# One fused attention and feed-forward kernel: where four pieces of side work stand in the order that is issued

## The chip, the cores and the metric

One core of one Trainium2 chip runs the whole program. The metric is device time in microseconds (us) of one execution, the median of several. Five engines work side by side, each through its own queue in order: TensorE (PE, whose weight loads are shown as PEld), VectorE (DVE), ScalarE (ACT), GpSimd (POOL) and SyncE (SP), which here issues all DMAs.

## The reference

`reference()` is causal attention followed by a gated feed-forward layer, all in float32:

```
scores = q @ k.T / sqrt(64); scores[future] = -1e9       # 4 batches, 12 heads, 448 tokens, 64 wide
x = (softmax(scores) @ v), heads side by side            # 1792 tokens x 768
xn = x / sqrt(mean(x*x) + 1e-6) * rms_g
g, val = xn @ w_gate, xn @ w_val                         # 768 -> 1536, twice
out = (g * sigmoid(g) * val) @ w_out                     # 1536 -> 768
```

The feed-forward weights come as 64-bit floats and are brought to float32 on the chip.

## The kernel before, in words

The tokens are worked on in three groups: 512 tokens (group 0), 512 (group 1) and 768 (group 2). Every product of the feed-forward part is made of three matmuls on split operands, high times high, high times low and low times high; a split is a copy that rounds (on ACT) and a subtraction (on DVE or POOL).

The program is issued by hand in small steps. `post(delay, fn)` puts a piece of work `delay` ticks later, `tick()` ends a tick, and what stands in an engine's queue is what these calls put there, in that order; nothing reorders it.

- Round 0 (`w_ = 0`): the feed-forward part of group 0, with the attention of group 1 strewn between.
- Round 1 (`w_ = 1`, us 258 to 532 of the profile): the feed-forward part of group 1, 36 units of 3 ticks each, so 108 ticks of six matmuls of 512 columns; the attention of group 2 is strewn between. That attention is 18 rounds of two attention units, each round 5 steps: a visit (scores of two later units, products with v of two earlier ones), then four steps `some(e)`, for two units and e = 0, 1: three or four transposes into the one PSUM bank `t` (L247) and the copy `pt` out of it (L251 on DVE, L253 on ACT). The 90 steps are spread evenly over the first `AT[1]` ticks, so where there are more steps than ticks, some ticks get two.
- Beside it in round 1, for each of 12 pairs of weight units, `quad_sums` (L405 to L408) makes four sums in place on DVE, in the tiles `w_r` that `split_w` (ACT `w_h`, then POOL `w_l`) reads first, and stores them to DRAM (L412). It is posted `T["ws"]` ticks after the split of the second unit.
- The chain of x (`x_steps`) starts on the tick after the attention's last: column sums, `rc`, diagonals `dg`, a matmul that spreads them, twelve scalings of the tiles `xq` (L514, DVE), sums `t` of them (L523, DVE), and the split of seven operands `ch`, `cl`. `todo` holds it, one entry per tick. The products for group 2 need all of it.
- The products with the gate and value weights for group 2 (`quad_product`, us 532 to 665), 7 instead of 8 products per weight, by sums of blocks.
- The last stage (us 665 to 746): 7 times 3 products with w_out (`out_product`), 18 matmuls of 384 columns each, results in a ring of two banks `s` or in held banks `m`, `x`. `out_result` reads a bank on DVE (L705) or ACT (L703); `h_operand` makes the next left operand `oh`, `ol`; `wo_load` brings w_out tiles in (L655, three DMAs each, four buffers) and `wo_split` splits them into `a_h` (ACT) and `a_l` (DVE).

Of the kernel before, what the change touches and what calls it, by code (L numbers as in the profile page):

```python
# [14 lines left out]
ALU = mybir.AluOpType  # L15
# [23 lines left out]
        for g in range(NG) for c in range(NP)}  # L39
# [1 line left out]
MASKED = -8.0e9  # L41


T = dict(c0=0, c1=1, c2=4, c20=9, c3=5, c30=10, c5=7, c50=14, exp=1, exp0=3, gt=1, hh=1, hl=4, ws=4,
         ld=4, ld1=11, lv=5, norm0=7, norm1=2, r1=5, so=3, wl=2, wl0=8, xl=2, xl0=9)
LOAD = (4, 12, 24, 36, 48, 60, 74)
CONVERT = (20, 32, 44, 62, 76)
# [3 lines left out]
WR = 4  # L51
WARM = [9, 0, 0, 2]
EXTRA = 4
AT = [108, 74]
XT = 768
HX = XT // 2
RING = 6
# [4 lines left out]
def attention_ffn(ctx: ExitStack, tc: tile.TileContext, qk0, qk1, qk2, v, v2, w, g, out, out2):  # L62
# [7 lines left out]
    nc = tc.nc  # L70
# [59 lines left out]
    def post(delay, fn):  # L130
        if delay <= 0:
            fn()
        else:
            later.setdefault(now[0] + delay, []).append(fn)
# [97 lines left out]
    def steps_t(p):  # L232

        if not 0 <= p < len(UNITS):
            return []
        _, kind, _, _, _, _ = UNITS[p]
        pr = hs[p]
        kb = KB[kind]

        def some(e):  # L240
            pt = pr["pt", e] = pt_p.tile([P, W], F32, tag=f"pt{e}", name="pt")
            ps = bank("x" if e and p < ENDS[1] + 1 else "t")
            at = 0
            for j in range(NKB[kind]):
                for o, wd in blocks(kind):
                    if kb * j < wd:
                        nc.tensor.transpose(ps[:kb, at: at + P],  # L247
                                            pr["sp"][e][:, o + kb * j: o + kb * (j + 1)], ident)
                        at += P
            if kind or (e and p < ENDS[0]):  # L250
                nc.vector.tensor_copy(pt[:kb, :at], ps[:kb, :at])  # L251
            else:
                nc.scalar.copy(pt[:kb, :at], ps[:kb, :at])  # L253

        return [lambda e=e: some(e) for e in (0, 1)]
# [146 lines left out]
    def quad_sums(v, t0, t1):  # L402

        a11, a12, a21, a22 = t0[:, : HX], t0[:, HX:], t1[:, : HX], t1[:, HX:]
        nc.vector.tensor_tensor(a22, a21, a22, op=ALU.add)  # L405
        nc.vector.tensor_tensor(a21, a11, a21, op=ALU.subtract)
        nc.vector.tensor_tensor(a11, a22, a11, op=ALU.subtract)
        nc.vector.tensor_tensor(a12, a12, a11, op=ALU.subtract)  # L408

        def store():  # L410
            for d, t in ((wy[v][:, : HX], a11), (wy[v][:, HX:], a22), (wz[v][:, : HX], a21), (wz[v][:, HX:], a12)):
                nc.sync.dma_start(out=d, in_=t)  # L412

        post(2, store)


    m_ps = {}
# [63 lines left out]
    xc = {}  # L481

    def x_steps():

        sm = side["sm"]
        rc = sm.tile([P, 6], F32, name="rc")
        dg = sm.tile([P, 2, HX], F32, tag="p2", name="dg").rearrange("p a (b c) -> p (a b) c", c=P)
        rb = {}

        def columns():  # L490
            ps = bank("t")[:, :6]
            for i in range(6):
                nc.tensor.matmul(ps[:, i: i + 1], acc[2, i // 3][:, P * (i % 3): P * (i % 3 + 1)],
                                 ones[:, :1], start=True, stop=True)
            nc.scalar.activation(rc, ps, AF.Sqrt, bias=eps, scale=1.0 / DM)
            post(1, lambda: nc.vector.reciprocal(rc, rc))

        def diagonal():
            for i in range(6):
                r = rc[:, i: i + 1]  # L500
                if i % 2:
                    nc.scalar.mul(dg[:, i], ident, r)
                else:
                    nc.gpsimd.tensor_scalar(dg[:, i], ident, r, 1.0, op0=ALU.mult, op1=ALU.mult)

        def spread():
            for j in (0, 1):
                rb[j] = bank("xy"[j])[:, :HX]
                nc.tensor.matmul(rb[j], ones, dg[:, 3 * j: 3 * j + 3].rearrange("p a b -> p (a b)"),
                                 start=True, stop=True)  # L510

        def scale(c, j):
            x = xr[2, c][:, HX * j: HX * (j + 1)]
            nc.vector.scalar_tensor_tensor(  # L514
                out=x, in0=x, scalar=g_sb[:, c: c + 1], in1=rb[j], op0=ALU.mult, op1=ALU.mult)

        tmp = {}

        def blk(k, j, c):
            return xq[c][:, k, HX * j: HX * (j + 1)]  # L520

        def sub(dst, a, b):
            nc.vector.tensor_tensor(dst, a, b, op=ALU.subtract)  # L523

        def sums(c):
            t12 = sm.tile([P, 2, HX], F32, tag=f"p{c}", name="t12")
            t1, t2 = t12[:, 0], t12[:, 1]
            t4 = sm.tile([P, HX], F32, tag=f"t4{c}", name="t4")
            sub(t1, blk(0, 1, c), blk(0, 0, c))
            sub(t2, blk(1, 1, c), t1)  # L530
            sub(blk(0, 1, c), blk(1, 1, c), blk(0, 1, c))
            sub(t4, blk(1, 0, c), t2)
            tmp[c] = t1, t2, t4

        def operand(i, c):
            if c == 0:
                xc[i] = tuple(side["xc"].tile([P, 3, HX], F32R, name=f"{n}{i}") for n in ("ch", "cl"))
            t1, t2, t4 = tmp.get(c, (None,) * 3)
            src = (blk(0, 0, c), t2, blk(1, 0, c), t1, blk(0, 1, c), blk(1, 1, c), t4)[i]
            split(xc[i][0][:, c], xc[i][1][:, c], src, i not in (0, 2, 5))  # L540

        todo = [[columns], [], [diagonal], [], [spread], []]
        for c in range(3):
            todo.append([lambda c=c, j=j, q=q: scale(q, j) for q in (c, c + 3) for j in (0, 1)])
            todo.append([lambda c=c, i=i: operand(i, c) for i in (0, 2, 5)])
        todo += [[lambda c=c: sums(c)] for c in range(3)]
        todo += [[lambda i=i, c=c: operand(i, c) for c in range(3)] for i in (1, 3, 4, 6)]
        return todo


# [98 lines left out]
    def wo_load(n):  # L649
        if n >= 21:  # L650
            return
        i, sl = divmod(n, 3)
        t = wr_p.tile([P, 2, 3, P], F32, tag="w", name="w_o")
        for m in range(3):
            nc.sync.dma_start(out=t[:, :, m], in_=WSRC[i](m).rearrange("p (k m) -> p k m", m=P)[  # L655
                :, 2 * sl: 2 * sl + 2])
        wt["o", n] = t

    def wo_split(n):
        if n >= 21:  # L660
            return
        f2["o", n] = ring(8 * NF // 2 + n)
        split(*f2["o", n], wt["o", n].rearrange("p a b c -> p (a b c)"), True)
# [99 lines left out]
    with tc.manual_schedule():  # L763
# [145 lines left out]
        for q in range(1, 4):  # L909
            h_operand(q)  # L910
        wo_split(5)
        for q in range(21):
            i, p = divmod(q, 3)
            ps_ = out_product(i, p)
            out_result(i, p, ps_)
            h_operand(q + 4)
            wo_load(3 * (i + 2) + p)
            if p == 2:
                for n in range(3):
                    wo_split(3 * (i + 2) + n)  # L920


# [46 lines left out]
```

## Time and profile before

| | |
|---|---|
| runs of before | 754.33, 757.47, 756.74 us; median 756.74 |
| profiled execution | 751.23 us, of which its span (first to last instruction) is 749.2 |
| mean granted TensorE clock in it | 0.974 of full speed |
| busy shares | PE 91%, weight loads 74%, DVE 71%, ACT 50%, POOL 49% |
| DMA | 138.80 MB, mean 185 GB/s |

Busy times of engines are counted in the span; a value in square brackets at the end of an instruction's row is the time its engine idled before it, and who released it. A granted clock of 1.00 is 2.4 GHz, 0.50 is 1.2 GHz.

### The profile page before, as it was taken

How to read it: one execution, taken by the hardware profiler on the slowest of the kernel's cores; microseconds unless marked ns; L12 is line 12 of the kernel's file. 1: busy time of each engine (PE TensorE's matmuls, PEld its weight loads, DVE VectorE, ACT ScalarE, POOL GpSimd, SP SyncE). 2: the span in 40 equal slices, each digit the busy share in tenths (PEclk: the TensorE clock that was granted, in tenths of full speed). 3: DMA queues.
4: the chain of work that ended last, by engine and by line, in shares of the span. 5: the costliest groups of instructions: out<-in, count | busy, mean ns of one | idle time of the engine just before them, and what ended most of it. 6: DMA issues, size and time to landing. Idle time of an engine off the chain costs nothing. (4 is left out here: it accounts for less than half of the span.)

```text
span 749.2 us, 11965 instructions
## 1 busy us (share of the span) xinstructions
PE 682.7 (91%) x4106; PEld 556.4 (74%) x4106; DVE 535.4 (71%) x1023; ACT 373.0 (50%) x832; POOL 369.1 (49%) x319
## 2 busy tenths in 40 slices
PE   8798899999999978879789889997999999998877
PEld 5465677777778655656566667875999999998877
DVE  5976899999987657566667656275386767698662
ACT  6868777778745443434235343334333343354340
POOL 4987345556666336263546455686254534411010
PEclk9999899999999999999899999998999999999898
DMA  8645677877785565555465645314557576443431
GB/s 276 230 154 171 203 257 248 282 255 267 253 309 177 159 219 151 179 164 185 153 190 180 199 160 151 121 57 133 176 190 256 177 251 232 138 127 104 118 95 63
DMA packets 71355, 138.80 MB, mean 185 GB/s; under 512 B 7744, under 2 KB 39232, under 8 KB 71296
## 3 DMA queue, kind: packets, MB, share of 16 engines
q1 hardware_dynamic: 71296, 138.05, 56.4%
q8 instruction: 32, 0.52, 0.3%
q14 instruction: 27, 0.22, 0.1%
HBM read 104.21 MB, written 33.82 MB: 184 GB/s over the span
## 5 line engine op out<-in xcount | busy, mean ns | idle before, releaser
L207 POOL TENSOR_SCALAR sp<-sp,rs 128x384 f32<-128x384 f32 (+3 forms) x132 | 82.9, 646 | 127.9 <-DVE rs L211 123.1
L433 PE MATMUL m_ps<-xh,w_h 128*128 128x512 f32 x282 | 122.5, 434 | 3.0 <-DVE t_sb L457 3.0
L202 ACT ACTIVATE sp<-sp,nm 128x384 f32<-128x384 f32 (+3 forms) x168 | 87.5, 524 | 52.7 <-DVE nm L199 51.2
L435 PE MATMUL m_ps<-xh,w_l 128*128 128x512 f32 x282 | 113.3, 402 | 0.0
L434 PE MATMUL m_ps<-xl,w_h 128*128 128x512 f32 x282 | 112.9, 400 | 0.0
L102 POOL TENSOR_TENSOR a_l<-w_q,a_h 128x768 fp32r<-128x768 f32 x24 | 47.2, 1965 | 66.9 <-ACT a_h L473 66.8
L247 PE MATMUL t_ps<-ident,sp 128*128 128x128 f32 (+1 forms) x309 | 52.6, 283 | 27.6 <-DVE pt L251 14.4
L102 POOL TENSOR_TENSOR w_l<-w_r,w_h 128x768 fp32r<-128x768 f32 x36 | 71.5, 1994 | 12.1 <-ACT w_h L387 10.5
L247 PEld LDWEIGHTS t_ps<-ident,sp 128*128 128x128 f32 (+1 forms) x309 | 36.9, 140 | 47.2 <-POOL sp L207 18.9
L251 DVE COPY pt<-t_ps 128x384 f32<-128x384 f32 (+1 forms) x71 | 42.5, 599 | 37.8 <-PE t_ps L247 37.6
L273 PEld LDWEIGHTS a_ps<-pt,v_r 128*64 128x64 f32 (+1 forms) x864 | 40.9, 138 | 37.9 <-issue 13.4
L273 PE MATMUL a_ps<-pt,v_r 128*64 128x128 f32 (+2 forms) x864 | 56.4, 269 | 12.6 <-DVE pt L251 8.4
L433 PEld LDWEIGHTS m_ps<-xh,w_h 128*128 128x128 f32 x282 | 54.6, 194 | 14.5 <-DVE t_sb L457 3.0
L373 POOL TENSOR_SCALAR w<-w 128x768 f32<-128x768 f32 x36 | 43.9, 1219 | 40.9 <-ACT w_c L372 35.0
L435 PEld LDWEIGHTS m_ps<-xh,w_l 128*128 128x128 f32 x282 | 54.4, 193 | 12.6
L199 DVE CUSTOM_DVE_ANT_0 sp<-s_ps,mask 128x128 f32<-128x128 f32 (+3 forms) x136 | 49.9, 416 | 18.4 <-PE s_ps L190 17.5
L435 PE MATMUL m_ps<-hh,w_l 128*128 128x512 f32 x144 | 57.8, 401 | 4.8 <-POOL w_l L102 4.8
L434 PEld LDWEIGHTS m_ps<-xl,w_h 128*128 128x128 f32 x282 | 54.9, 195 | 8.1
L433 PE MATMUL m_ps<-hh,w_h 128*128 128x512 f32 x144 | 59.2, 411 | 0.0
L434 PE MATMUL m_ps<-hl,w_h 128*128 128x512 f32 x144 | 57.2, 397 | 0.0
L377 DVE SCALAR_TENSOR_TENSOR w_c<-w_c,w 128x768 int32<-128x768 int32 x36 | 51.2, 1422 | 0.5
L102 POOL TENSOR_TENSOR w_l<-w_c,w_h 128x768 fp32r<-128x768 f32 x18 | 40.0, 2222 | 22.5 <-ACT w_h L387 22.5
(178 smaller groups left out, 1698.4 us busy)
## 6 DMA issues: line engine op xcount, KB each, us to landing
w<-in_w SPq DMA_DIRECT2D x36, 768.0 KB, 5.2
w<-w_c SPq DMA_DIRECT2D x36, 384.0 KB, 2.6
w_r<-w SPq DMA_DIRECT2D x36, 384.0 KB, 4.7
qk_r<-in_qk SPq DMA_DIRECT2D x48, 256.0 KB, 4.4
qk_r<-in_qk SPq DMA_DIRECT2D x12, 512.0 KB, 5.9
v_r<-in_v SPq DMA_DIRECT2D x12, 448.0 KB, 4.5
v_r<-in_v SPq DMA_DIRECT2D x24, 192.0 KB, 3.1
wy<-w_r SPq DMA_DIRECT2D x24, 192.0 KB, 2.9
```

Of the source, the lines that this page charges most:

```text
L102: nc.gpsimd.tensor_tensor(out_, a, b, op=op)
L199: nc.vector.tensor_tensor_reduce(out=sp, in0=ps, in1=mk, scale=nsc, scalar=3.0e38, op0=ALU.add, op1=ALU.min, accum_out=nm)
L202: post(T["exp" if p >= ENDS[0] else "exp0"], lambda: nc.scalar.activation(sp, sp, AF.Exp, bias=nm, scale=-1.0, accum_out=sm))
L207: pr["norms"].append(lambda: nc.gpsimd.tensor_scalar(sp, sp, rs, 1.0, op0=ALU.mult, op1=ALU.mult))
L247: nc.tensor.transpose(ps[:kb, at: at + P], pr["sp"][e][:, o + kb * j: o + kb * (j + 1)], ident)
L251: nc.vector.tensor_copy(pt[:kb, :at], ps[:kb, :at])
L273: nc.tensor.matmul(av_ps[e * D: (e + 1) * D, p % 2, q0: q0 + n], raw_v[p][:kb, h, j, e, :], pr["pt", e][:kb, a0: a0 + n], start=(j == 0), ...
L373: (T["c1"], lambda: nc.gpsimd.tensor_scalar(hf_, hf_, 0.0, 1.0, op0=ALU.mult, op1=ALU.mult)),
L377: (T["c3" if s >= 5 else "c30"], lambda: nc.vector.scalar_tensor_tensor(out=ti, in0=ti, scalar=3, in1=lo, op0=ALU.logical_shift_left, op1= ...
L433: nc.tensor.matmul(ps, wh[:, k, :], mh, start=(first and k == ks[0]), stop=False)
L434: nc.tensor.matmul(ps, wh[:, k, :], ml, start=False, stop=False)
L435: nc.tensor.matmul(ps, wl[:, k, :], mh, start=False, stop=(last and k == 5))
```

## The change

Four edits, none of which adds or removes arithmetic.

1. `quad_sums` posts its four sums one a tick instead of issuing them together; `ws` goes from 4 to 3, so the first comes a tick sooner and the last two ticks later; the stores are posted after the last.
2. In group 2 the copies `pt` with e = 0 go to ACT (36 of 72); e = 1 stay on DVE.
3. `AT[1]` goes from 74 to 82, so group 2's attention takes 82 of the 108 ticks, and the chain of x starts 8 ticks later. Its entries are cut anew: operands are split one a tick beside the scalings and sums, not three in a tick.
4. In the last stage the w_out tiles of round i + 3 are loaded at the end of round i, after its splits; before, those of round i + 2 were loaded one at a time through round i.

```diff
-T = dict(... hl=4, ws=4,
+T = dict(... hl=4, ws=3,
-AT = [108, 74]
+AT = [108, 82]
...
-            if kind or (e and p < ENDS[0]):
+            if (kind and e) or (e and p < ENDS[0]):
                 nc.vector.tensor_copy(pt[:kb, :at], ps[:kb, :at])
             else:
                 nc.scalar.copy(pt[:kb, :at], ps[:kb, :at])
...
-        nc.vector.tensor_tensor(a22, a21, a22, op=ALU.add)
-        nc.vector.tensor_tensor(a21, a11, a21, op=ALU.subtract)
-        nc.vector.tensor_tensor(a11, a22, a11, op=ALU.subtract)
-        nc.vector.tensor_tensor(a12, a12, a11, op=ALU.subtract)
+        todo = [(a22, a21, a22, ALU.add), (a21, a11, a21, ALU.subtract),
+                (a11, a22, a11, ALU.subtract), (a12, a12, a11, ALU.subtract)]
+        for d, (o, x, y, op) in enumerate(todo):
+            post(d, lambda o=o, x=x, y=y, op=op: nc.vector.tensor_tensor(o, x, y, op=op))
...
-        post(2, store)
+        post(4, store)
...
-        for c in range(3):
-            todo.append([lambda c=c, j=j, q=q: scale(q, j) for q in (c, c + 3) for j in (0, 1)])
-            todo.append([lambda c=c, i=i: operand(i, c) for i in (0, 2, 5)])
-        todo += [[lambda c=c: sums(c)] for c in range(3)]
-        todo += [[lambda i=i, c=c: operand(i, c) for c in range(3)] for i in (1, 3, 4, 6)]
+        todo = [[columns], [], [diagonal], [], [spread], [], scales(0), scales(3),
+                scales(1) + op(0, 0), scales(4) + op(2, 0), scales(2) + op(5, 0), scales(5) + op(0, 1)]
+        for c, i, k in ((0, 2, 1), (1, 5, 1), (2, 0, 2)):
+            todo.append([lambda c=c: sums(c)] + op(i, k))
+        for i, x in ((1, op(2, 2)), (3, op(5, 2)), (4, []), (6, [])):
+            todo.append(op(i, 0) + op(i, 1) + op(i, 2) + x)
...
+        for n in (6, 7, 8):
+            wo_load(n)
         for q in range(21):
...
-            wo_load(3 * (i + 2) + p)
             if p == 2:
                 for n in range(3):
                     wo_split(3 * (i + 2) + n)
+                for n in range(3):
+                    wo_load(3 * (i + 3) + n)
```

On PE, in round 1, in the fourth of the 18 attention rounds, the six transposes of one unit (its halves e = 0 and e = 1) stood together; this is one piece of the difference.

```order
 L434 MATMUL m_ps<-xl,w_h 128x512
 L435 MATMUL m_ps<-xh,w_l 128x512
-L247 MATMUL t_ps<-ident,sp 128x128 x6
+L247 MATMUL t_ps<-ident,sp 128x128 x3
+L433 MATMUL m_ps<-xh,w_h 128x512
+L434 MATMUL m_ps<-xl,w_h 128x512
+L435 MATMUL m_ps<-xh,w_l 128x512
+L433 MATMUL m_ps<-xh,w_h 128x512
+L434 MATMUL m_ps<-xl,w_h 128x512
+L435 MATMUL m_ps<-xh,w_l 128x512
+L247 MATMUL t_ps<-ident,sp 128x128 x3
```

A tick's six matmuls now stand between the halves. Of the 18 rounds, four (the 4th, 6th, 13th and 15th) are parted so, and three more get a tick of matmuls at a place where the transposes had followed the visit, or the next visit them, at once; six rounds keep a pair of halves side by side.

On DVE, in the same stage, first before (the sums of the pair v = 3, in the fifth attention round), then of the change (the last sum of pair 2 and the first two of pair 3; all sums are line 408 there).

```order
L447 TENSOR_TENSOR gr<-m_ps,rms 128x512
L251 COPY pt<-t_ps 112x512
L405 TENSOR_TENSOR w_r<-w_r 128x384
L406 TENSOR_TENSOR w_r<-w_r 128x384
L407 TENSOR_TENSOR w_r<-w_r 128x384
L408 TENSOR_TENSOR w_r<-w_r 128x384
L211 RECIPROCAL rs<-sm 128x2 x2
L449 SCALAR_TENSOR_TENSOR t_sb<-t_sb,gr 128x512
L251 COPY pt<-t_ps 112x512 x3
```

```order
L408 TENSOR_TENSOR w_r<-w_r 128x384
L447 TENSOR_TENSOR gr<-m_ps,rms 128x512
L211 RECIPROCAL rs<-sm 128x2 x2
L449 SCALAR_TENSOR_TENSOR t_sb<-t_sb,gr 128x512
L251 COPY pt<-t_ps 128x384
L408 TENSOR_TENSOR w_r<-w_r 128x384
L447 TENSOR_TENSOR gr<-m_ps,rms 128x512
L251 COPY pt<-t_ps 128x384
L408 TENSOR_TENSOR w_r<-w_r 128x384
```

Four sums in a row ahead of the reciprocals and a copy have become single sums between them, and two of a round's four copies are gone from this queue.

On ACT, near the end of round 1, first before, then of the change: `w_h` is the split of a weight unit of round 1, `ch<-xq` and `ch<-t` are splits of the chain's operands (made of the scaled x and of its sums).

```order
L387 CAST w_h<-w_r 128x768
L473 CAST ch_5437<-xq 128x384 x3
L473 CAST ch_5451<-t_5358 128x384
L473 CAST ch_5451<-t_5371 128x384
L473 CAST ch_5451<-t_5390 128x384
L387 CAST w_h<-w_r 128x768 x2
```

```order
L473 CAST ch_5361<-xq 128x384
L387 CAST w_h<-w_r 128x768
L473 CAST ch_5471<-t_5419 128x384
L473 CAST ch_5471<-t_5434 128x384
L473 CAST ch_5471<-t_5449 128x384
L473 CAST ch_5379<-xq 128x384
```

Before, the last three `w_h` of the round stood behind splits that wait for the sums `t`; now the last `w_h` stands ahead of all of these.

## Rows read from the trace of the kernel before

**Rows 1.** Windows by stage: us; PE, PEld, DVE, ACT, POOL busy; clock; DMA share; GB/s.

```profile
258.00:476.90 218.90, 188.28 (x1458) 136.75 (x1458) 136.74 (x331) 87.75 (x215) 111.00 (x109) 0.98 0.53 171
476.90:531.80 54.90, 50.05 (x211) 40.28 (x210) 29.57 (x43) 19.34 (x37) 34.21 (x23) 0.94 0.34 108
531.80:665.40 133.60, 132.11 (x758) 130.81 (x757) 95.10 (x140) 54.57 (x90) 56.45 (x28) 1.00 0.61 201
665.40:745.60 80.20, 70.27 (x379) 69.05 (x377) 54.56 (x61) 29.73 (x42) 11.72 (x6) 0.94 0.33 97
```

**Rows 2.** Waits of PE, us 258 to 476.9: total, times, longest.

```profile
PE t_ps L247 <- DVE pt L251: 14.4, 10, 2.9
PE t_ps L247 <- POOL sp L207: 7.5, 6, 3.0
PE a_ps L273 <- DVE pt L251: 4.6, 1, 4.6
PE t_ps L247 <- DVE rs L211: 4.0, 3, 2.6
```

**Rows 3.** Timeline of PE, stalls of that stage: start, duration.

```profile
268.22 0.65 PE L247 MATMUL t_ps<-ident,sp 128*112 128x128 f32 x4 [3.03 <-POOL sp L207]
...
291.66 0.52 PE L247 MATMUL t_ps<-ident,sp 128*128 128x128 f32 x3 [2.63 <-DVE pt L251]
...
307.10 0.62 PE L247 MATMUL t_ps<-ident,sp 128*112 128x128 f32 x4 [2.77 <-DVE pt L251]
...
370.62 1.12 PE L273 MATMUL a_ps<-pt,v_r 128*64 128x128 f32 x8 [4.56 <-DVE pt L251]
```

**Rows 4.** Timeline of DVE ahead of the stall at 307.10.

```profile
303.30 0.55 DVE L405 TENSOR_TENSOR w_r<-w_r 128x384 f32<-128x384 f32 x1
...
305.06 0.56 DVE L408 TENSOR_TENSOR w_r<-w_r 128x384 f32<-128x384 f32 x1
...
306.27 0.68 DVE L251 COPY pt<-t_ps 112x512 f32<-112x512 f32 x1
```

**Rows 5.** Groups by line and shape: busy us, mean ns, idle before.

```profile
L251 DVE COPY pt<-t_ps 128x384 f32<-128x384 f32 x47 | 26.1, 554 | 26.5 <-PE t_ps L247 26.5
...
L406 DVE TENSOR_TENSOR w_r<-w_r 128x384 f32<-128x384 f32 x12 | 12.1, 1006 | 0.4
L253 ACT COPY pt<-t_ps 128x384 f32<-128x384 f32 x24 | 11.3, 469 | 7.8 <-PE t_ps L247 7.7
```

**Rows 6.** Waits of ACT, us 258 to 476.9.

```profile
ACT w_h L387 <- DMA w_r<-w: 21.2, 5, 6.0
ACT sq L304 <- POOL acc L102: 19.9, 4, 5.9
```

**Rows 7.** Timeline of POOL and PE, end of round 1.

```profile
511.30 9.18 POOL L102 TENSOR_TENSOR w_l<-w_r,w_h 128x768 fp32r<-128x768 f32 x3 [5.16 <-ACT w_h L387]
...
516.97 0.80 PE L435 MATMUL m_ps<-hh,w_l 128*128 128x512 f32 x1 [4.40 <-POOL w_l L102]
```

**Rows 8.** Timelines of DVE, PE and ACT, last stage.

```profile
694.10 0.96 DVE L475 TENSOR_TENSOR a_l<-w_o,a_h 128x768 fp32r<-128x768 f32 x1 [0.99 <-ACT a_h L473]
694.98 0.55 DVE L705 SCALAR_TENSOR_TENSOR u<-s_ps,m 128x384 f32<-128x384 f32 x1
...
729.71 0.96 DVE L475 TENSOR_TENSOR a_l<-w_o,a_h 128x768 fp32r<-128x768 f32 x1 [2.15 <-ACT a_h L473]
...
695.68 0.66 PE L572 MATMUL s_ps<-a_h,oh 128*128 128x384 f32 x1 [4.65 <-ACT oh L473]
...
731.29 0.66 PE L572 MATMUL s_ps<-a_h,oh 128*128 128x384 f32 x1 [5.03 <-ACT oh L473]
...
728.85 0.83 ACT L473 CAST a_h<-w_o 128x768 fp32r<-128x768 f32 x1 [2.37 <-DMA w_o<-wsum]
```

**Rows 9.** Windows behind two stalls: us, PE busy, granted clock, DMA share, GB/s.

```profile
371.00:374.00 3.00, 3.00 (x16) 0.50 1.00 309
517.00:520.60 3.60, 3.60 (x9) 0.50 0.70 207
```

More of the change, by code (lines that the diff above doesn't have):

```diff
@@ L41 @@
 MASKED = -8.0e9
-T = dict(c0=0, c1=1, c2=4, c20=9, c3=5, c30=10, c5=7, c50=14, exp=1, exp0=3, gt=1, hh=1, hl=4, ws=4,
+T = dict(c0=0, c1=1, c2=4, c20=9, c3=5, c30=10, c5=7, c50=14, exp=1, exp0=3, gt=1, hh=1, hl=4, ws=3,
          ld=4, ld1=11, lv=5, norm0=7, norm1=2, r1=5, so=3, wl=2, wl0=8, xl=2, xl0=9)
@@ L535, in operand @@
         def operand(i, c):
-            if c == 0:
+            if i not in xc:
                 xc[i] = tuple(side["xc"].tile([P, 3, HX], F32R, name=f"{n}{i}") for n in ("ch", "cl"))
@@ L540, in operand, with scales, op @@
             split(xc[i][0][:, c], xc[i][1][:, c], src, i not in (0, 2, 5))
-        todo = [[columns], [], [diagonal], [], [spread], []]
-        for c in range(3):
-            todo.append([lambda c=c, j=j, q=q: scale(q, j) for q in (c, c + 3) for j in (0, 1)])
-            todo.append([lambda c=c, i=i: operand(i, c) for i in (0, 2, 5)])
-        todo += [[lambda c=c: sums(c)] for c in range(3)]
-        todo += [[lambda i=i, c=c: operand(i, c) for c in range(3)] for i in (1, 3, 4, 6)]
+        def scales(q):
+            return [lambda j=j: scale(q, j) for j in (0, 1)]
+        def op(i, c):
+            return [lambda: operand(i, c)]
+        todo = [[columns], [], [diagonal], [], [spread], [], scales(0), scales(3),
[4 more added lines that the diff above has]
+            todo.append(op(i, 0) + op(i, 1) + op(i, 2) + x)
         return todo
```

## The prediction

> **What bounds the kernel now.** I read the busy shares by stage first. TensorE is busy 188.3 of 218.9 us in round 1, 50.1 of 54.9 at its end, 132.1 of 133.6 in the products for group 2 and 70.3 of 80.2 in the last stage [rows 1]. No other engine is near full in any of them, so the time is TensorE's own work and the places where TensorE stands still, and a change that adds no arithmetic can only work on the second. The waits of TensorE and its timeline give those places.
>
> In round 1 they come to 14.4 + 7.5 + 4.6 + 4.0 = 30.5 us [rows 2]. In most of them a set of transposes waits for the copy that empties the one bank `t`, or the products with v wait for such a copy. The stall of 2.77 us that ends at 307.10 shows the cause [rows 3]: the first of two adjoining sets was done, and DVE came to its copy only at 306.27, after four weight sums that ran from 303.30 to 305.62 [rows 4]. The 4.56 us that end at 370.62 have the same burst in front, lengthened: the second sum of a burst takes 1.006 us in the mean [rows 5], though one by itself takes 0.56 [rows 4].
>
> At the end of round 1 TensorE waits 4.40 us for POOL's low part of a weight, on which POOL had started after 5.16 us of waiting for ACT's high part [rows 7]. ACT had it behind splits of the chain of x, which waited for DVE's sums.
>
> In the last stage there are two stalls, 4.65 and 5.03 us [rows 8]. The rows name ACT's `oh`, but that operand had been ready; what ended last is DVE's reading of the ring bank (`u` at 694.98), and this stood behind the split of a w_out tile that waited 0.99 us for ACT, the second time 2.15 us; there ACT waited 2.37 us for the tile's DMA [rows 8].
>
> Behind a long stall the granted clock is 0.50 for some us [rows 9], so a stall can cost more than its own length: at half speed half of each busy us is lost.
>
> **The change part by part.** *Copies, sums and spacing in round 1 (edits 1, 2 and the 82 ticks).* These three meet the same 30.5 us, so they are costed together. A copy of 128x384 out of the bank takes 469 ns on ACT and 554 on DVE [rows 5], so 36 moved copies give DVE some 36 x 0.55 = 20 us of time back in a stage where it is busy 136.7 us, and cost ACT 17 where it is busy 87.8 [rows 1]. This is worth nothing by itself; what counts is when the copy comes. By kind:
>
> - Waits for DVE's copies, 14.4 + 4.6 = 19.0 us in 11 places [rows 2]. In four rounds the halves now have a tick of matmuls between them, which covers a copy; I take these as gone. At about seven places I leave the turn of one copy with its semaphores, about 0.7 us: an estimate from the copy's 0.554 [rows 5]. That leaves 4.9; recovered 14.
> - Waits for POOL's normalized scores and for DVE's reciprocals, 7.5 + 4.0 = 11.5 us in 9 places [rows 2]. This is a latency, scores to minimum to exponential to reciprocal to POOL. Three rounds get a tick more before the transposes that need it, the one with 3.03 us [rows 3] among them, and the reciprocals no longer stand behind bursts. I take 4.5 as recovered; the bounds are 0 and 8.
> - New waits. On ACT the copies stand behind what holds that queue: in this stage 5 waits of 21.2 us in all for a weight's DMA, and 4 of 19.9 us for POOL's accumulation [rows 6]. Going through the order of ACT, the copy of a round's second unit stands behind the second square in six of 18 rounds, and in two of them its transposes are a tick early; the waits for a DMA mostly end after a round's copies. The stores, and so the weights that reuse their buffers, come a tick later, but in the SP queue more weight loads now stand ahead of the loads of v that block it. With sums one tick sooner, DVE can also wait longer for POOL to have read the tile. I charge 3 us; the bounds are 0 and 12, the second being half the time that ACT is held, at the most part of one copy each.
>
> Sum 14 + 4.5 - 3 = 15.5. TensorE ran about 3 us at half clock behind the 4.56 us stall [rows 9], and somewhat behind another: 1.5 more if these stalls go.
>
> *Weight against the sums.* Bursts of 0.55 us instructions were stretched only while POOL ran: the mean of the second sum is 1.006 us [rows 5]. Spread out, each of the four meets POOL by itself, and POOL is busy 111.0 of 218.9 us [rows 1], so one or two of four will meet it, as now; I charge nothing beyond the 3 us. The Trainium skill, "SBUF — State Buffer", section "SBUF: two separate sides", says the ports that DVE and POOL share are an exclusive lock, held for a whole instruction. By that a spread burst can lose the lock up to four times where a burst mostly loses it twice: 11 bursts x 2 x 0.45 = 10 us more of DVE's time, an estimate, and if all of it reached TensorE, a gain of 16 in place of the sum's. The rows agree with it in kind.
>
> *The chain of x (edit 3).* It starts 8 ticks later and must be ready at the end of tick 108. A tick takes (54.9 - 4.4 - 1.8) / 33 = 1.5 us there [rows 1, 7, 9], so from its first entry at tick 84 there are 25 ticks, some 37 us; before, there were 33. DVE's part does not get shorter: twelve scalings and twelve sums, and its order is the same. What is gained is the order on ACT: the last `w_h` stands ahead of the splits that wait for the sums. POOL's last `w_l` still follows the last split of its operands, for which ACT waits for the sums of c = 2. I put that end at tick 106 or so, just when TensorE wants it, and leave 0.8 of 4.8 us: 4.0 recovered, bounds -3 and 4.8. Behind the 4.40 us stall 3.6 us were run at half clock [rows 9]: of the 1.8 lost, 1.5 back.
>
> *The w_out loads (edit 4).* The waits for DMA leave both chains: DVE's `u` or `c` comes 0.99 us sooner in the first stall and 2.15 in the second [rows 8], so 3.1 of 9.7. The rest stays: DVE has three `a_l` and ACT three `a_h` in front of the reading of the bank, and their order is unchanged. I add 0.3 for the clock. A load issued a round sooner needs a buffer whose split is a round old, so it doesn't block SP for long; the results' stores behind it are waited for by nobody until the end.
>
> Sum: 15.5 + 1.5 + 4.0 + 1.5 + 3.1 + 0.3 = 25.9 us. Against the profiled execution, 751.23, that is 725.3. That execution was 5.5 us faster than the median of the runs, 756.74, from which the forecast is taken: 756.74 - 25.9 = 730.8, so **731**.
>
> **The rivals.** *The copies on ACT come late.* Where ACT is held for a DMA or for POOL [rows 6], a copy behind it holds bank `t`, and TensorE. For it: 41 us of such holds. Against: most fall after a round's copies. At the upper bound 12 in place of 3, and with nothing recovered from the latency waits, 13.5 less: a gain of 12, **744**.
>
> *The stage is bound by its latency.* Each round goes scores, exponential, normalization, transposes, copy, products, and TensorE's wait moves to the next link when one is shortened. For it: waits for POOL and reciprocals are already 11.5 us, and two of the four in rows 2 are not for a copy. Against: the largest have a burst right in front. Then round 1 gives 3, the rest half of 9: a gain of 7, **750**. The change would then have done little of what it says.
>
> *The other side: sums that meet POOL one by one.* 44 sums stand in this stretch; if each waits for a POOL instruction as the second does now (1.006 against 0.56), DVE gets 44 x 0.45 = 20 us of waits, now in front of minima, reciprocals and the e = 1 copies in every tick instead of every third round, and a first sum that comes a tick sooner waits for `w_l`. It decides if more than some 60% of these 20 us reach TensorE on top of the old 30.5 with nothing recovered there; with the later chain of x costing 3: +12 + 3 - 3 = 12 slower, **769**. Short of that it only eats the gain.
>
> The lock of the Trainium skill's page named above is this rival's mechanism; the stretched rows bear it out for a burst, and none shows it for single sums.
>
> **How the numbers follow.** Forecast (722 to 740) 0.60, late copies (740 to 748) 0.20, latency (748 to 756) 0.13, the other side (over 757) 0.07. 8 in 10 lie between 721 and 750: the low end is the sum with the bounds of 8 for the latency waits and no new waits, 756.74 - 32.4 = 724, and a few us for the spread of the runs; the high end takes in the first two rivals. About 0.5% (3.8 us) is what a measurement can tell from no change; faster than 753: 0.60 + 0.20 + half of the third, 0.86; within: 0.08; slower: 0.06.
>
> **What would show it right or wrong.** Right: in the stage of round 1 TensorE's waits for L251 fall from 19 us to about 5, with a few small ones for ACT's L253; the 4.40 us wait for `w_l` falls under 1; the two stalls of the last stage are still there, of about 3.6 and 2.9 us, with no wait for a w_out DMA in front. Wrong: waits for L253 of 2 us and more behind a `w_h` or a square; sums of over 1 us in every place; a start of the group 2 products that waits for `cl`; stalls of the last stage that vanish or stay whole.

## The result, and the profile after

The changed kernel takes 729.25 us (median of 4 runs, 726.92 to 730.18), the kernel before in the same job 756.1 (4 runs, 754.33 to 757.47): a ratio of 0.9642, 95% interval 0.961 to 0.9673. The forecast was 731. The profiled execution took 730.18 us (span 728.1, clock 0.984) against 751.23, so the traces have 21.05 of the 26.9 us to show; the execution of before that was profiled was 5 us faster than its median.

Windows of the kernel after, by stage: us; PE, PEld, DVE, ACT, POOL busy; clock; DMA share; GB/s.

```profile
258.00:466.40 208.40, 196.56 (x1520) 144.08 (x1519) 116.18 (x303) 106.55 (x253) 119.37 (x114) 1.00 0.58 189
466.40:507.10 40.70, 35.89 (x161) 28.88 (x160) 29.07 (x39) 16.64 (x33) 24.80 (x19) 1.00 0.27 88
507.10:645.90 138.80, 134.22 (x757) 132.38 (x758) 98.42 (x144) 54.37 (x90) 57.46 (x28) 0.99 0.61 203
645.90:724.60 78.70, 72.06 (x379) 70.85 (x378) 54.45 (x62) 29.31 (x42) 11.73 (x6) 0.91 0.34 98
```

Against [rows 1], round 1 with its end is 24.7 us shorter (it ends at 507.1, not 531.8), the products for group 2 are 5.2 longer, the last stage 1.5 shorter. The first two windows can only be added: the attention now takes 8 more of the 108 ticks, so the border lies elsewhere in the work. The clock of 0.98 in round 1 is 1.00 now; that of the last stage fell from 0.94 to 0.91.

Waits of TensorE after, us 256 to 458.2, the attention's stretch of round 1: total, times, longest.

```profile
PE t_ps L247 <- ACT pt L253: 8.5, 11, 1.7
PE t_ps L247 <- POOL sp L207: 2.6, 3, 1.3
PE t_ps L247 <- DVE pt L251: 1.9, 2, 1.0
```

They answer to [rows 2]: 13.0 us in place of 30.5. None is longer than 1.7 us, and the waits of 2.6 to 4.6 us [rows 3] are gone. Of what is left, 8.5 us are for the copies that now run on ACT.

Groups of the weight sums, of before and then of after: busy us, mean ns, idle before.

```profile
L405 DVE TENSOR_TENSOR w_r<-w_r 128x384 f32<-128x384 f32 x12 | 10.2, 848 | 5.6 <-POOL w_l L102 5.6
L407 DVE TENSOR_TENSOR w_r<-w_r 128x384 f32<-128x384 f32 x12 | 8.3, 692 | 0.4
L408 DVE TENSOR_TENSOR w_r<-w_r 128x384 f32<-128x384 f32 x12 | 7.4, 615 | 0.4
```

```profile
L408 DVE TENSOR_TENSOR w_r<-w_r 128x384 f32<-128x384 f32 x48 | 32.9, 686 | 13.6 <-POOL w_l L102 9.0 <-DMA qk_r<-in_qk 2.6 <-DMA v_r<-in_v 1.7
```

With L406 of [rows 5] the 48 sums took 38.0 us in bursts. One at a time they take 32.9, a mean of 0.686 us: spread out they lost less to POOL, not more. (In either trace 12 of the 48 are stretched beyond 0.65 us, all of them beside a POOL instruction; in the bursts they were stretched further.)

Waits of ACT after, the same stretch, as in [rows 6].

```profile
ACT sq L304 <- POOL acc L102: 11.2, 4, 4.3
ACT w_h L387 <- DMA w_r<-w: 6.9, 4, 3.9
```

ACT is held for 18.1 us there, not 41.1.

Timeline of TensorE after: the stalls of over 2 us behind the attention (start, duration, in brackets the idle time before and its releaser).

```profile
500.88 0.50 PE L435 MATMUL m_ps<-hh,w_l 128*128 128x512 f32 x1 [2.50 <-POOL w_l L102]
...
507.16 0.66 PE L578 MATMUL m_ps<-ch,a_h 128*128 128x384 f32 x1 [2.37 <-DVE ob L441]
...
514.60 0.44 PE L578 MATMUL m_ps<-ch,a_h 128*128 128x384 f32 x1 [2.60 <-ACT m L601]
...
675.12 0.66 PE L578 MATMUL s_ps<-a_h,oh 128*128 128x384 f32 x1 [3.56 <-DVE u L711]
...
708.95 0.66 PE L578 MATMUL s_ps<-a_h,oh 128*128 128x384 f32 x1 [2.78 <-DVE c L711]
```

The first three stand where before there were 4.40 [rows 7] and 0.45 us: 7.47 in all, more than before. The third is already inside the products for group 2, and a stretch at half clock (below) lies there too: with 1.6 us for that, they are 4.2 of the 5.2 us by which the stage grew. The last two answer to [rows 8], 4.65 and 5.03 us.

Timeline of DVE after, chain of x.

```profile
477.63 0.69 DVE L441 SCALAR_TENSOR_TENSOR ob<-m_ps,rms 128x512 f32<-128x512 f32 x1 [9.25 <-PE m_ps L435]
...
495.56 7.81 DVE L475 TENSOR_TENSOR cl<-t,ch 128x384 fp32r<-128x384 f32 x6
503.29 3.12 DVE L475 TENSOR_TENSOR cl<-xq,ch 128x384 fp32r<-128x384 f32 x3
506.33 0.68 DVE L441 SCALAR_TENSOR_TENSOR ob<-m_ps,rms 128x512 f32<-128x512 f32 x1
506.94 1.48 DVE L475 TENSOR_TENSOR cl<-t,ch 128x384 fp32r<-128x384 f32 x3
508.34 0.95 DVE L475 TENSOR_TENSOR a_l<-w_q,a_h 128x768 fp32r<-128x768 f32 x1
```

Timeline of POOL after, the same place.

```profile
495.74 1.25 POOL L102 TENSOR_TENSOR cl<-xq,ch 128x384 fp32r<-128x384 f32 x1 [4.98 <-ACT ch L473]
497.40 1.34 POOL L102 TENSOR_TENSOR cl<-xq,ch 128x384 fp32r<-128x384 f32 x1 [0.41 <-ACT ch L473]
498.70 2.12 POOL L102 TENSOR_TENSOR w_l<-w_r,w_h 128x768 fp32r<-128x768 f32 x1
500.79 4.27 POOL L102 TENSOR_TENSOR a_l<-w_q,a_h 128x768 fp32r<-128x768 f32 x2
...
515.35 1.85 POOL L102 TENSOR_TENSOR a_l<-w_q,a_h 128x768 fp32r<-128x768 f32 x1 [10.29 <-ACT a_h L473]
```

What matters here is the overlap. From 495.74 to 505 POOL splits with one pause of 0.41 us, and DVE's six splits of sums, which take 0.49 us each in the three at 506.94, take 1.30 each, 7.81 in all. The result of the last tick, `ob` at 506.33, stands behind nine of them, and TensorE's first product for group 2 waits for it. The copy into `m`, the third wait, stands on ACT behind a split that waited for its tile's DMA:

```profile
513.65 0.51 ACT L473 CAST a_h<-w_q 128x384 fp32r<-128x384 f32 x1 [11.64 <-DMA w_q<-w]
```

Timeline of DVE after, last stage.

```profile
670.79 3.71 DVE L475 TENSOR_TENSOR a_l<-w_o,a_h 128x768 fp32r<-128x768 f32 x3 [0.88 <-ACT a_h L473]
674.43 0.54 DVE L711 SCALAR_TENSOR_TENSOR u<-s_ps,m 128x384 f32<-128x384 f32 x1
...
704.57 3.77 DVE L475 TENSOR_TENSOR a_l<-w_o,a_h 128x768 fp32r<-128x768 f32 x3
708.26 0.55 DVE L711 SCALAR_TENSOR_TENSOR c<-s_ps,u 128x384 f32<-128x384 f32 x1
```

No DMA stands in front of either stall any more. The bank's reading (`u`, `c`) stands behind three splits of w_out, and the rows of TensorE now name it.

The whole stretches at half clock, of after and then of the last stage of before: us; PE, PEld, DVE, ACT, POOL busy; clock; DMA share; GB/s.

```profile
506.94:510.35 3.41, 3.19 (x10) 3.22 (x11) 2.95 (x6) 0.00 (x0) 0.00 (x0) 0.50 0.64 193
674.19:681.01 6.82, 5.89 (x18) 5.92 (x19) 2.98 (x5) 0.08 (x1) 0.00 (x0) 0.50 0.62 163
708.32:715.15 6.83, 6.20 (x19) 6.23 (x20) 2.75 (x6) 0.00 (x0) 0.00 (x0) 0.50 0.16 58
```

```profile
693.70:700.52 6.82, 4.84 (x15) 4.88 (x16) 3.63 (x5) 1.84 (x3) 0.00 (x0) 0.50 0.64 179
731.24:734.66 3.42, 3.37 (x11) 3.40 (x12) 2.10 (x3) 0.00 (x0) 0.00 (x0) 0.50 0.32 115
```

Each begins inside a stall and outlasts it; TensorE then runs at 1.2 GHz. If half of its busy time there counts as lost (an estimate), that is 1.6, 2.9 and 3.1 us after, and 2.4 and 1.7 us in the last stage before.

### The profile page after: what moved, and what is told of

The parts are those of the page before. It is cut to its first block, busy times and chain, and to the rows that moved or that the text cites. A ratio compares the mean times of both kernels' runs of the same rounds, so it can differ in the third digit from the quotient of the medians.

```text
span 728.1 us, 11977 instructions
## 1 busy us (share of the span) xinstructions
PE 678.3 (93%) x4106; PEld 553.2 (76%) x4106; DVE 512.6 (70%) x987; ACT 387.6 (53%) x868; POOL 366.6 (50%) x319
## 5 line engine op out<-in xcount | busy, mean ns | idle before, releaser
L435 PE MATMUL m_ps<-xh,w_l 128*128 128x512 f32 x282 | 111.6, 396 | 0.0
L102 POOL TENSOR_TENSOR a_l<-w_q,a_h 128x768 fp32r<-128x768 f32 x24 | 48.8, 2034 | 65.8 <-ACT a_h L473 65.6
L102 POOL TENSOR_TENSOR w_l<-w_r,w_h 128x768 fp32r<-128x768 f32 x36 | 68.0, 1895 | 23.0 <-ACT w_h L387 22.3
L253 ACT COPY pt<-t_ps 128x384 f32<-128x384 f32 (+1 forms) x60 | 29.6, 494 | 44.0 <-PE t_ps L247 44.0
L102 POOL TENSOR_TENSOR w_l<-w_c,w_h 128x768 fp32r<-128x768 f32 x18 | 39.3, 2183 | 24.1 <-ACT w_h L387 21.3
L375 DVE SCALAR_TENSOR_TENSOR w<-w 128x768 int32<-128x768 int32 x36 | 46.3, 1287 | 6.8 <-POOL w L373 6.7
```

Of the source, the lines that this page charges most:

```text
L102: nc.gpsimd.tensor_tensor(out_, a, b, op=op)
L375: (T["c2" if s >= 5 else "c20"], lambda: nc.vector.scalar_tensor_tensor(out=lo, in0=lo, scalar=29, in1=hi, op0=ALU.logical_shift_right, op ...
L435: nc.tensor.matmul(ps, wl[:, k, :], mh, start=False, stop=(last and k == 5))
```

## The experiments

The theory: in round 1 the waits were copies behind bursts and tight spacing, and the three edits share the gain; at its end DVE's splits, slowed by POOL, took the place of the late weight; in the last stage the reading behind three splits remains. The rivals: one edit does it all; the entries of the chain do help and something else was lost; w_out loads do nothing. "Waits" below are TensorE's, from the profile of each run, in the attention's stretch and in the stretch of the chain (to the first products, the wait for `m` with it). After has 13.0 and 7.47.

**Attention in 74 ticks again.**

```diff
-AT = [108, 82]
+AT = [108, 74]
```

> The changed kernel with the attention of group 2 back on 74 ticks; the chain of x then starts at tick 76 as before. Theory (three edits share the gain of round 1, and the late chain of x costs 5 to 7 us): TensorE's waits in the attention stretch rise from 13 us to about 20, for the parted halves and the extra ticks are gone; the three waits at the start of the group 2 products (2.50, 2.37 and 2.60 us) shrink to under 2 in all, so the two nearly cancel: 730 us, between 726 and 735. Rival (the 82 ticks carry the gain of round 1): the waits return to 25 us or more and the time is 740 or more.

Measured: 737.28 us (736.29 to 738.73), ratio 0.9744 [0.9713, 0.9775]. Waits 21.2 and 5.3. So the 82 ticks are worth 8 us, not 1; the expectation had set them too low, and the rival's condition, waits of 25 us or more, did not come either. The later chain costs 2.2 us of waits, and the attention gives back 8.2. The other edits without the ticks still gain 19 us on the kernel before.

**82 ticks alone, on the kernel before.**

```diff
-AT = [108, 74]
+AT = [108, 82]
```

> The kernel before with only the 82 ticks. Theory (sharing): waits of TensorE in the attention stretch fall from 30 to about 21, with bursts still in front of the longest; the later chain of x, in its old order, costs 5 or more at the start of the group 2 products, so 752 us, between 747 and 757. Rival (the 82 ticks carry the gain): 735 to 742.

Measured: 753.03 us (748.14 to 756.11, 12 runs), ratio 0.9954 [0.9925, 0.9982]. Waits of the attention 27.9, against 30.5 before; the two largest rows:

```profile
PE t_ps L247 <- DVE pt L251: 18.9, 9, 4.7
PE t_ps L247 <- DVE rs L211: 4.0, 2, 3.5
```

The same ticks give some 3 us where the bursts and DVE's copies still stand: spacing alone leaves most of the waits for an engine whose queue holds a burst.

**The sums in a burst again.**

```diff
-T = dict(... ws=3,
+T = dict(... ws=4,
...
-        todo = [(a22, a21, a22, ALU.add), (a21, a11, a21, ALU.subtract),
-                (a11, a22, a11, ALU.subtract), (a12, a12, a11, ALU.subtract)]
-        for d, (o, x, y, op) in enumerate(todo):
-            post(d, lambda o=o, x=x, y=y, op=op: nc.vector.tensor_tensor(o, x, y, op=op))
+        nc.vector.tensor_tensor(a22, a21, a22, op=ALU.add)
+        nc.vector.tensor_tensor(a21, a11, a21, op=ALU.subtract)
+        nc.vector.tensor_tensor(a11, a22, a11, op=ALU.subtract)
+        nc.vector.tensor_tensor(a12, a12, a11, op=ALU.subtract)
...
-        post(4, store)
+        post(2, store)
```

> The changed kernel with the four sums of a pair issued together again, first sum at 4 ticks, stores 2 later, as before. Theory (bursts on DVE delay copies, minima and reciprocals): TensorE's waits in the attention stretch rise from 13 us to about 19, the longest over 2 us behind a burst: 735 us, between 732 and 741. Rival (with half the copies on ACT the bursts have nothing urgent behind them, the spread does nothing): 729, between 726 and 731.

Measured: 738.31 us (736.51 to 744.35), ratio 0.977 [0.973, 0.981]. Waits 19.9 and 9.3. The row of TensorE's waits that grew most, and what ACT waits for most in that stretch:

```profile
PE t_ps L247 <- ACT pt L253: 14.8, 13, 2.8
ACT sp L202 <- DVE nm L199: 39.3, 13, 6.3
```

The copies are on ACT here, and still wait for the bursts: DVE's minima `nm` come late, so the exponentials on ACT (39.3 us of waits, 24.0 after), so the copies behind them. Spreading the sums is worth 9 us.

**All copies on DVE again.**

```diff
-            if (kind and e) or (e and p < ENDS[0]):
+            if kind or (e and p < ENDS[0]):
```

> The changed kernel with all copies of group 2 back on DVE. Theory (the copies gain little by moving, since on ACT they stand behind exponentials; what matters is spacing and spread sums): the 11 waits for ACT's copies, 8.5 us, are replaced by about as many for DVE's: 730 us, between 727 and 734. Rival (the move to ACT is what frees DVE): waits of 20 us and more in the stretch, 738 or more.

Measured: 732.07 us (730.69 to 734.13), ratio 0.9673 [0.9638, 0.9707]. Waits 14.4 and 8.8, of the first 11.2 for L251. The moved copies are worth about 3 us. The intervals of this run and of after overlap, so the sign is likely and the size open.

**The old w_out loads.**

```diff
-        for n in (6, 7, 8):
-            wo_load(n)
...
+            wo_load(3 * (i + 2) + p)
...
-                for n in range(3):
-                    wo_load(3 * (i + 3) + n)
```

> The changed kernel with the w_out loads one at a time through the round again. Theory (the loads took 0.99 and 2.15 us out of the two stalls of the last stage, but the half clock behind the second grew longer): the stalls are 4.7 and 5.0 us again, and half speed behind the second covers under 1 us of work in place of 4; the last stage is 1.6 us longer: 731, between 729 and 733. Rival (the clock behind a stall costs the same whatever its length): 3.3 us longer: 733.

Measured: 734.66 us (732.36 to 735.71), ratio 0.9714 [0.968, 0.9748]. Its stalls came back as 4.52 and 4.99 us, with ACT waiting again for the tile:

```profile
675.64 0.83 ACT L473 CAST a_h<-w_o 128x768 fp32r<-128x768 f32 x1 [2.16 <-DMA w_o<-wsum]
...
711.56 0.83 ACT L473 CAST a_h<-w_o 128x768 fp32r<-128x768 f32 x1 [2.48 <-DMA w_o<-wsum]
```

That is 5.4 us slower than after and beyond both forecasts. The last stage took 80.6 us against 78.7: 3.2 us more of stalls, less some 1.3 of clock, since half speed covers 5.7 and 3.9 us of work behind them, not 5.9 and 6.2. The theory's 1 us behind the second stall did not come; it rested on too short a reading of the trace of before (below). Another 2.0 us stand in the profile ahead of that stage, where this edit moves nothing. Most of that is clock too: two stretches at half speed with 3.4 us of work each (502.85 to 506.26 and 516.50 to 519.91), where after has one with 3.2. Why the second came is open.

**The chain of x in its old entries, still 8 ticks later.**

```diff
-        todo = [[columns], [], [diagonal], [], [spread], [], scales(0), scales(3),
...
+        todo = [[columns], [], [diagonal], [], [spread], []]
+        for c in range(3):
+            todo.append([lambda c=c, j=j, q=q: scale(q, j) for q in (c, c + 3) for j in (0, 1)])
+            todo.append([lambda c=c, i=i: operand(i, c) for i in (0, 2, 5)])
+        todo += [[lambda c=c: sums(c)] for c in range(3)]
+        todo += [[lambda i=i, c=c: operand(i, c) for c in range(3)] for i in (1, 3, 4, 6)]
```

> The changed kernel, 82 ticks, with the entries of the chain of x as they were before. Theory (the new order frees ACT's last high parts of weights, so without it POOL's low part is late again): a wait of 4 us and more for POOL's low part and the same waits for the chain behind it: 734 us, between 730 and 740. Rival (the entries' order does nothing, the 8 ticks set the waits): 729, between 727 and 731.

Measured: 726.63 us (723.99 to 731.12), ratio 0.9613 [0.957, 0.9656]; waits 13.4 and 4.8. My theory fell: the new entries gain nothing, and TensorE waits 2.7 us longer with them (the times' intervals overlap; the waits show it). The wait for POOL's low part, 4.40 us before, is 1.1 here with the old entries, as it is with the 82 ticks alone, so the later start takes most of it away by itself. Here POOL does its splits earlier, beside DVE's sums, and stands still from 498.67 to 505.70. DVE's rows:

```profile
496.88 2.20 DVE L523 TENSOR_TENSOR xq<-xq 128x384 f32<-128x384 f32 x1
499.01 0.55 DVE L523 TENSOR_TENSOR t<-xq,t 128x384 f32<-128x384 f32 x1
...
501.47 2.89 DVE L475 TENSOR_TENSOR cl<-t,ch 128x384 fp32r<-128x384 f32 x6
```

Six splits take 2.89 us beside an idle POOL, and 7.81 after. But seven sums take 1.27 to 2.20 each beside a busy one: the entries choose which of DVE's instructions pay.

**The chain sooner: the spread one tick earlier, the scalings on the next tick.**

```diff
-        todo = [[columns], [], [diagonal], [], [spread], [], scales(0), scales(3),
+        todo = [[columns], [], [diagonal], [spread], scales(0), scales(3),
```

> The changed kernel with the chain's spread one tick sooner and the scalings on the tick behind it, so 2 ticks sooner in all, ahead of a result that DVE waits 9 us for. Theory (DVE stood idle for that result, and so its scalings, sums and operand splits came 5 us late and held the last results of round 1): the scalings start at about 472 us in place of 478, and the three waits of 2.50, 2.37 and 2.60 us shrink to under 2.5 in all: 723 us, between 719 and 727. Rival (the splits end late because POOL stretches them, 7.81 us for six, whenever they start): 728, between 726 and 731.

Measured: 728.6 us (727.96 to 732.0), ratio 0.9644 [0.9609, 0.9679]; waits 13.3 and 6.6. The scalings start 4.5 us sooner than after (473.75, not 478.24), and `ob` comes 0.15 us sooner, because of this row of DVE:

```profile
492.30 9.50 DVE L475 TENSOR_TENSOR cl<-t,ch 128x384 fp32r<-128x384 f32 x6
```

The rival was right: a sooner start only gives the splits more time beside POOL.

**The w_out splits behind the next round's bank readings.**

```diff
+            if i and p == 0:
+                wo_split(3 * (i + 1))
+            if i and p == 1:
+                for n in (1, 2):
+                    wo_split(3 * (i + 1) + n)
+                for n in range(3):
+                    wo_load(3 * (i + 2) + n)
             if p == 2:
-                for n in range(3):
-                    wo_split(3 * (i + 2) + n)
-                for n in range(3):
-                    wo_load(3 * (i + 3) + n)
```

> The changed kernel with the three splits of w_out tiles of a round issued after the bank readings of the next round's first and second product, not ahead of them. Theory (what is left of the two stalls, 3.56 and 2.78 us, is a reading of the ring bank on DVE behind three splits): both stalls shrink to under 1 us, and with them some 3 us of half speed: 723 us, between 720 and 727. Rival (DVE has more work there than time, the order only moves the wait): waits of the same sum for operands or splits, 728 to 732.

Measured: 726.03 us (724.18 to 730.15), ratio 0.9607 [0.9569, 0.9645]. TensorE's waits in the last stage are 3.6 us, 3.0 less than after:

```profile
PE s_ps L578 <- ACT a_h L473: 2.0, 2, 1.2
PE s_ps L578 <- DVE a_l L475: 1.4, 2, 0.7
```

This shows what the two stalls of after were: the bank's reading behind three splits. (The loads move with the splits, two products later.) The stage took 73.8 us against 78.7; the rest goes with the clock, which differs from run to run there (last section).

**Both that gained: old entries, and w_out splits late.** The edits are the last two of those above (the entries of the chain, the splits) in one kernel.

> After, with two of the edits that gained: the chain of x in its old entries, and the splits of w_out behind the next round's bank readings. The two touch stages that lie 160 us apart. Alone they gave 726.6 and 726.0 against 729.25, so 2.6 and 3.2 us. Theory, the two add up: 723.4, between 721 and 726, with 5 us of waits in the stretch of the chain and 3.7 in the last stage. Rival, the old entries gave nothing and the difference of 2.6 was the spread of the runs: 726.

Measured: 722.86 us (719.35 to 725.5), ratio 0.9559 [0.9526, 0.9592]; waits 13.4 and 5.0, last stage 70.7 us with 3.6 of waits and no half clock in it. They add up, and the 3 us of the old entries came a second time. The interval lies clear of that of after (0.961 to 0.9673), so the gain of both is shown; each alone overlaps it.

**After, with later stores of group 1's results.**

```diff
-so=3,
+so=8,
```

> After, with the stores of group 1's results eight ticks behind their bank readings, not three. Theory: in the changed kernel the store that waits for the reading of the last tick stands in SP's queue ahead of the loads of the first block weights, and the 2.6 us in which TensorE waits for ACT's copy into m at 514.6 come from there, so ACT's wait of 11.6 us for a DMA shrinks to a few us, that wait of TensorE goes, and the time falls by 2 to 3: 726.5, between 725 and 728. Rival: the loads wait for their buffers, or the wait only moves to the next link (the low part on POOL or DVE), and the time stays at 729.

Measured: 733.22 us (731.86 to 738.53), ratio 0.9716 [0.9681, 0.975]: 4 us slower, and the theory fell. Rows of its SP, DVE and ACT timelines:

```profile
512.66 0.95 DVE L475 TENSOR_TENSOR a_l<-w_q,a_h 128x768 fp32r<-128x768 f32 x1
...
513.63 0.32 SPq L564 DMA_DIRECT2D w_q<-w  x1
...
517.65 0.90 SPq L443 DMA_DIRECT2D out_t<-ob  x2
...
520.54 0.48 ACT L601 COPY m<-m_ps 128x384 f32<-128x384 f32 x1 [3.88 <-DMA out_t<-ob]
```

SP still issues a block's load only at 513.63, right after DVE's `a_l` (512.66 + 0.95) has read the buffer: the loads wait for DVE's queue, not for the store. And the copy into `m` now waits for the store, 3.88 us, which holds the tile that `m` takes: TensorE waits 5.9 us for it.

**The best kernel (both that gained) with the later stores.** The same edit on it.

> The kernel of the first run of this job (old entries of the chain, w_out splits late) with the stores eight ticks behind. Theory: where the old entries stand, TensorE waited only 0.6 us for that copy and 1.9 for the bank reading, so the later stores give 0.5 to 1 us here: 722.8, between 721 and 725. Rival: with the loads out of the way the last bank reading is early too, 720.

Measured: 725.52 us (724.65 to 729.42), ratio 0.9612 [0.9581, 0.9643]; 2.7 us slower, with overlapping intervals, and with the same wait in its trace: TensorE waits 4.2 us for ACT's copy, which waits 3.89 for a store.

**The best kernel with the attention in 78 ticks.**

```diff
-AT = [108, 82]
+AT = [108, 78]
```

> The kernel of the first run of this job with the attention in 78 ticks in place of 82. From 74 to 82 ticks the stretch of the attention gave 8.9 us less waiting (21.9 to 13.05) and the stretch of the chain cost 2.2 more. Theory, the gain is about even over the ticks: 4.4 us more waiting in the attention, 1.1 to 2.5 less behind it, so 725.7, between 724 and 728. Rival: what the 8 ticks buy is bought by the first four, and the chain that starts sooner gains 2: 721.

Measured: 723.04 us (722.78 to 726.0, 5 runs), ratio 0.9582 [0.955, 0.9613]. Waits 14.0 and 5.0: from 74 to 82 ticks the changed kernel's waits fell by 8.2 us (the expectation has 8.9), and here the first four ticks leave only 0.6 of that to the last four, as the rival had it; the sooner chain gains nothing, against both. The time is that of 82 ticks.

## Why the prediction was right, by its steps

**Round 1: 15.5 us of waits, measured 17.5** (30.5 to 13.0). The mechanism is shown: two of the three edits, undone, cost 8 and 9 us, the copies likely 3, and 82 ticks without the other two give only 3. Two sizes were off and partly cancelled. Copies: 19.0 to 10.4 us (8.5 for L253 and 1.9 for L251), so 8.6 recovered, where 14 less 3 of new waits, 11, stood. Latency: 11.5 to 2.6, so 8.9 in place of 4.5, beyond the bound of 8; minima, exponentials and reciprocals too had waited behind the bursts. The 1.5 us for the clock were low: half speed covered 307.99 to 311.40 and 369.43 to 376.26 us of before, with 9.05 us of TensorE's work, so some 4.5 were lost, and none is left. (The view in [rows 9] ends at 374.00, inside the second stretch, so "about 3 us" was 5.6.) ACT's holds of 41 us, the ground of the first rival, shrank to 18.1. The second rival, a wait that only moves to the next link, is out with the fall to 13.0; so is the third: the sums are stretched less.

**The chain of x: 4.0 + 1.5 us gained, measured 2.6 lost in waits and 1.4 gained in clock.** The step that failed is "DVE's part does not get shorter", which took it as no longer either. The `w_l` wait shrank from 4.40 to 2.50, not to 0.8, and two new waits came: 2.37 for `ob` behind DVE's nine splits, and 2.60 for ACT's copy into `m`. The sum had no price for those splits, though the new entries put POOL's splits and its last `w_l` beside them; the old entries and the sooner start show that POOL's work beside DVE sets the length. The order on ACT did what was forecast: at 74 ticks the new entries leave 0.56 us of the `w_l` wait. But TensorE then waits 4.72 for `ob`. What holds the copy into `m` is ACT's `a_h` ahead of it, which waited 11.6 us for a load whose buffer DVE frees late. The bound of -3 held. The clock came out as forecast by chance: half speed behind the 4.40 us stall ran to 523.03, not 520.6, with 6.1 us of work, and 3.2 are left.

The Trainium skill, "SBUF — State Buffer", section "SBUF: two separate sides", says that a DVE instruction with two SBUF inputs and a POOL instruction that reads SBUF exclude each other for a whole instruction. The trace agrees: a split of DVE that takes 0.55 us by itself (0.49 from start to start) lasts 1.36 to 2.20 beside POOL, about as long as the POOL instruction it meets (1.25 to 2.16). Two of the six, beside POOL's of 1.34 and 2.12 us above:

```profile
497.80 1.36 DVE L475 TENSOR_TENSOR cl<-t,ch 128x384 fp32r<-128x384 f32 x1
499.08 2.16 DVE L475 TENSOR_TENSOR cl<-t,ch 128x384 fp32r<-128x384 f32 x1
```

The page gives no price for these instructions; the forecast cited it for the sums, where it cost less than in bursts, and not for these splits, where it cost 4.9 us (7.81 against 2.89 for six).

**The last stage: 3.1 us from the waits, 3.3 measured; 0.3 from the clock, 1.9 lost.** Stalls of 3.6 and 2.9 were forecast, and 3.56 and 2.78 came; that `oh` in the rows of before stood for the bank's reading is shown by the late splits. But before, the half clock covered 4.8 and 3.4 us of work behind the stalls, and in the trace of after 5.9 and 6.2. The stage gained 1.5 us there. The loss is of this execution and not of the edit: other runs with the same stalls lost less (last section).

**The sum.** Waits 17.5 - 2.6 + 3.3 and clock 4.5 + 1.4 - 1.9 make 22.2 where the traces differ by 21.05; taking half of the busy time as lost to the clock is somewhat too much. By the windows alone, TensorE's idle time from 258 us to the end of its work fell by 19.0 us and its busy time by 2.0. The traces show 21.05 of the 25.9 us forecast, mostly because the chain lost where it was to gain. That the forecast from the median (731) came so near owes something to the cancelled sizes, and something to luck: the execution profiled before was faster than that kernel's median, and the one after was the slowest of its four, so medians differ by more than the traces.

## What to carry to other kernels

A burst on one engine delays whatever stands in the chain behind it, on other engines too: spread it, and give the chain the ticks; the ticks alone gave 3 us here, the other edits without them 19 of the 27. Before moving two-input instructions of DVE, look at what POOL does beside the new place, and price them at the stretched rows. When a stall in front of a bank goes, ask which other instructions stand between the bank and its reading; moving those took 3.0 us of waits off, as much again as taking away the DMA wait ahead of them (3.3). And before pricing a stall's clock, read the granted clock to the end of the slow stretch: views that ended too soon made the prediction's clock terms too small.

## What the runs showed of the hardware that was not expected

The length of a stall did not tell what it cost in clock. The second stall of the last stage, 2.77 or 2.78 us, is the same in seven runs whose instructions there are the same. At half speed behind it TensorE did 6.2 us of work (after, and 74 ticks), 6.0 (later stores), 3.4 (old entries; the chain sooner), 2.8 (all copies on DVE) and none (sums in a burst). The 5.03 us of before were followed by 3.4. Windows behind that stall, of after and of the run with the burst:

```profile
708.95:715.15 6.20, 6.20 (x19) 6.20 (x20) 2.12 (x4) 0.00 (x0) 0.00 (x0) 0.50 0.18 63
...
720.61:727.00 6.39, 6.39 (x37) 6.39 (x38) 2.60 (x4) 0.00 (x0) 0.00 (x0) 1.00 0.26 92
```

So the last stage of these seven took from 74.6 to 78.7 us, with the same two stalls. A difference of two or three us between single profiles can be clock alone; compare the waits, and the medians.

Two engines pay unequally for the same collision. DVE's splits go from 0.55 to as much as 2.20 us each, while POOL's 768-column splits go from 1.85 us with DVE idle to between 2.12 and 2.16.

A store can delay a copy through its source tile: the late stores held the tile of `ob` that `m` takes next, 3.9 us in two kernels.
